# Kernel units that write one half of their products in reverse order, so that one VectorE copy collects a unit's results in place of two

## The chip, the cores and the metric

The kernel runs on one core of one Trainium2 chip. The metric is the device time of one execution in microseconds, taken as the median of the runs shown.

## What is computed

A tensor x of 2048 rows and 512 columns goes through two pairs of layers. Layer A is a two-dimensional Fourier filter, layer B a long convolution whose kernel K is built from complex exponentials. Cut to what matters:

```python
def _A_ref(x, w_r, w_i):
    X = rfft2(x) * (w_r + 1j * w_i)
    return irfft2(X, s=(S, D))

def _B_ref(u, A_re, A_im, B_re, B_im, C_re, C_im, log_dt, Dskip):
    dt = exp(log_dt)[:, None]
    logdA, dB, Cc = dt * (A_re + 1j * A_im), dt * (B_re + 1j * B_im), C_re + 1j * C_im
    P = exp(logdA[:, :, None] * arange(L)[None, None, :])
    K = einsum("dn,dnl,dn->dl", Cc, P, dB).real        # 512 channels, 128 states, 2048 taps
    y = irfft(rfft(pad(K)) * rfft(pad(u)))[:, :L]
    return y.T + u * Dskip

x = x + A(layernorm(x)); x = x + B(layernorm(x))
x = x + A(layernorm(x)); x = x + B(layernorm(x))
```

K does not depend on x, so it is built once and serves both B layers.

## The kernel before

The work is cut into small pieces, written as Python generators that yield the engine and the tile slots they want next. A planner, the class Clock, runs them on a model of the engines while the program is written: in each step it takes, among the pieces that could start within NEAR = 0.1 us of the earliest, the one with the lowest rank, lets it emit its next instructions, and charges them to the engine by the table COST (line 40). The order in which instructions stand in each engine's queue is what this planner chose. Two details of its model bear on the change: on GpSimd an element counts 2.12 ns, or 1.77 ns where no operand has more than one dimension longer than one (lines 365 to 367), and on VectorE 1.05 ns after a fixed 0.07 us. Where the model sees TensorE idle, the planner puts in filler matmuls (line 427) into a free PSUM bank.

There are two planner runs. The first (line 1379) interleaves the building of K with the first A layer; the second (line 1387) holds everything else.

K is built in 32 **kernel units** (unit_k, line 1237), each for 16 channels. Every time index is 64 times a coarse index plus or minus a fine one, so the exponentials are products of a first factor E1 (32 columns for each of 16 channels) and a second factor E2 with two halves h of 32 columns. In steps, with the lines:

1. TensorE forms phases in a two-bank PSUM tile p (lines 1244, 1245). ScalarE rounds them (1247), VectorE subtracts (1249) and takes the absolute value (1250), ScalarE takes two sines (1252, 1253): cosines into the SBUF tile c, sines back into p.
2. The magnitudes m come from exp_k (line 1233), 48 instructions on ScalarE.
3. The tile E holds real parts E[:, 0] and imaginary parts E[:, 1], each of 1536 columns: 512 for E1, 512 for half 0 and 512 for half 1 of E2. VectorE writes the imaginary parts (line 1260 for the first 1024 columns, line 1261 for half 1 with a minus sign), GpSimd the real parts (line 1264 for 1024 columns, line 1265 for half 1 with 512 columns).
4. TensorE multiplies E1 by E2 (line 1277: 32 products in the code, 64 in the trace) into a one-bank PSUM tile pk of kind "l". The kinds l, t, h and x share two such banks, so this tile competes with the folds and the inverse transforms of layer A for a place.
5. VectorE copies the 256 results of a partition from pk into KS, a buffer of 64 positions by 32 channels (lines 1284 to 1289). There are two copies of 128 columns, because half 0 belongs to the positions 32 to 63 in ascending order and half 1 to the positions 31 to 0 in descending order.
6. After eight units store_k (line 1291) writes KS to memory by four DMAs on SyncE's queue, and turn_k (line 1301) reads it back, transposes it and sends it on. There is one KS buffer; there are two E buffers.

The two lines that make the two copies:

```python
        for h, l in enumerate((slice(32, 64), slice(31, None, -1))):
            nc.vector.tensor_copy(KS[u // 8][:, l, o:o + 4].rearrange("p l e -> p e l"), k[:, :, h])
```

Beside the units, in the same planner run, layer A goes on: forward_a (line 581), first_a (line 710) with folds on TensorE (fold_d, line 636), products on VectorE (lines 744 to 746), one sum on GpSimd (line 750) and one on VectorE (line 752), and inv_a (line 776), whose sums stand on GpSimd (lines 803, 804) and whose results VectorE adds to x (lines 814, 816) before it takes their moments (540, 541). At the end norm_b (line 836) normalizes x for the first B layer (line 566). spectra_k (line 906) takes the spectrum of the finished part of K (lines 903, 925, 927).

Some pieces wait for the planner's own events: spread (line 544) for the moments of its rows, the copies that overwrite the folded buffer (lines 698, 772) for earlier folds. SBUF is cut by hand: one tensor wk of WORK columns holds rings of small buffers, of which RING1 serves the first planner run and RING2 the second.

Of the kernel before, what the change touches and what calls it, by code (L numbers as in the profile page):

```python
# [11 lines left out]
OP = mybir.AluOpType  # L12
# [1 line left out]
RING1 = {"co": (1024, 3), "si": (1024, 2), "oh": (1280, 1), "KS": (2048, 1), "KT": (512, 4), "yh": (512, 2), "gb": (256, 3), "st": (256, 2), "sk": (128, 1)}  # L14

RINGW = {"y": (516, 2), "d": (258, 3), "c": (256, 3), "a": (512, 2)}
RING2 = {"gi": (512, 8), "kh": (1024, 4), "yk": (1024, 2), "gk": (256, 2), "iy": (1024, 2)}

BANKS1, SAME1 = {'a': (0, 2, 4), 's': (6, 7)}, {'t': 's', 'h': 's', 'l': 's', 'x': 's', 'k': 'a'}
BANKS2 = {'x': (0, 1, 2, 3), 't': (4, 5), 'h': (6, 7), 'a': (0, 2, 4, 6), 'f': (0, 2)}  # L20
# [27 lines left out]
PACE = 0, 1  # L48
LATE = 1, 1
HOLD = 4  # L50
NEAR = 0.1
FILL = 1.5, 0.6, 0.22
LANES = 8

WORK = 16896


PSUM = bass.MemoryType.PSUM
# [135 lines left out]
class Clock:  # L194
# [4 lines left out]
    def __init__(self, net, last=None):  # L199
        self.net, self.n = net, len(net.nc.cur_bb.bb.instructions)  # L200
        self.free, self.seen, self.events, self.marks, self.drops = {}, {}, {}, [], []
        self.held, self.slots, self.land, self.piece, self.table, self.form = {}, {}, 0.0, None, "", None
        self.pools, self.lands, self.lanes = [], [], {}
        if last:
            self.lands = last.lands
            self.free, self.seen, self.events, self.land, self.table = last.free, last.seen, last.events, last.land, last.table

# [221 lines left out]

    def run(self, plan):  # L430

        pieces = [[rank, i, 0.0, (), piece] for i, (rank, piece) in enumerate(plan)]
        while pieces:
            ready = [(t, p) for p in pieces if (t := self.time(p[2], p[3])) is not None]
            assert ready, [p[4].__name__ for p in pieces]
            now = min(t for t, _ in ready) + NEAR
            t, p = min((e for e in ready if e[0] <= now), key=lambda e: e[1][:2])
            if any(isinstance(need, str) and "PE" in need.split() for need in p[3]):
                self.fill(t)
            self.piece = p[4]  # L440
            needs = next(p[4], self)
            end = self.note(t)
            if not (isinstance(needs, str) and needs[:1] == "+"):
                p[2] = end
            if needs is self:
                pieces.remove(p)
                self.drops += [k for k, h in self.held.items() if h[2] is p[4] and k not in self.drops]
            else:
                p[3] = needs if isinstance(needs, tuple) else () if needs is None else (needs,)
            self.release()  # L450


class Net:
# [81 lines left out]
    def moments(self, s2, st):  # L535

        nc = self.nc
        self.stat(st, s2 // 4)
        b = self.sm.tile([128, 6], F32, name="st")
        nc.vector.bn_stats(b, self.x[:, s2, :])  # L540
        nc.vector.bn_aggr(st[s2 // 4][0][:, s2 % 4, :], b)
        self.mark("moments", id(st), s2 // 4)

    def spread(self, i, st, act=False, half=None):

        yield "ACT", self.after(("moments", id(st), i), 4 if half is None else 2 * half + 2)
        mv, rs = (a if half is None else a[:, 2 * half:2 * half + 2] for a in st[i][:2])
        self.nc.scalar.activation(rs, mv[:, :, 1], AF.Sqrt, bias=1e-5)
        yield "DVE"
        self.nc.vector.reciprocal(rs, rs)  # L550
        if act:
            if len(st[i]) < 3:
                st[i] = *st[i], self.sm.tile([128, 4], F32, name="nb")
            b = st[i][2] if half is None else st[i][2][:, 2 * half:2 * half + 2]
            self.nc.vector.scalar_tensor_tensor(b, mv[:, :, 0], -1.0, rs, op0=OP.mult, op1=OP.mult)
        self.mark(*(k for k in (id(st), i, half) if k is not None))
# [74 lines left out]
    def fold_d(self, p, r, g):  # L631

        cs = p.rearrange("p (a b) -> p a b", a=2)
        for b, o in enumerate((cs[:, :, 0:64], cs[:, :, 64:128], p[:, 128:256], p[:, 384:512])):
            y = 2048 * b + 128 * g
            self.nc.tensor.matmul(o, self.Yf[r][:, y:y + 128], self.Da[:, b, :], start=True, stop=True)
        self.mark("fold", r)

    def group_a(self, g):

        nc = self.nc
# [8 lines left out]
        p = self.psum("t")  # L650
# [44 lines left out]
        for sg in range(2):  # L695
            nc.tensor.matmul(v[:, 2 + sg], Z[:, sg, 129:257], H[sg], start=True, stop=True)
        self.drop(Z, G)
        yield "ACT", self.emitted(("fold", 1), g // 4 * 4)
        nc.scalar.copy(Y1[:, 0:2], v[:, 0:2].rearrange("p b (s m) -> p b s m", s=16))
        P, M = (v[:, 2 + sg].rearrange("p (r s u) -> p r s u", r=2, s=16) for sg in range(2))  # L700
        yc, ys = Y1[:, 2:4, :, 0:4], Y1[:, 2:4, :, 4:8]
# [8 lines left out]
    def first_a(self, r, g):  # L710

        nc = self.nc
# [8 lines left out]
        p = self.psum("t")  # L721
# [36 lines left out]
        for b in range(2):  # L758
            o = v[:64, 128 * b:128 * b + 128]
# [3 lines left out]
            o = v[64:, 128 * b:128 * b + 128]  # L763
# [5 lines left out]
            nc.tensor.matmul(v[:, 256:512], Z[:, i, 129:257], ca[:, o:o + 2].rearrange("p a m -> p (a m)"),  # L769
                             start=i == 0, stop=i == 1)  # L770
        self.drop(Z, G)
        yield "ACT", self.emitted(("fold", r), g // 4 * 4)
        nc.scalar.copy(Y1, v.rearrange("p (b s m) -> p b s m", b=4, s=16))
        self.mark("group", r)

# [154 lines left out]
    def tables(self):  # L930

        for q in range(8):
            yield "+SP gi", self.emitted(("sent", 0), HOLD * (q > 1))
            self.gi[q] = self.w("gi", [128, 2, 8, 32])
# [131 lines left out]
    def moments_b(self, s2, e, st):  # L1066

        nc = self.nc
        yield "DVE", self.after(("summed", 0, e), self.returns(0, e)), self.emitted(("half", s2), e)
        if ("h", s2 // 4) not in st:  # L1070
            st["h", s2 // 4] = self.sm.tile([128, 4, 2, 6], F32, name="hm")
        m = st["h", s2 // 4][:, s2 % 4]
        nc.vector.bn_stats(m[:, e], self.x[:, s2, 256 * e:256 * e + 256])
        if e:
            nc.vector.bn_aggr(self.stat(st, s2 // 4)[:, s2 % 4, :], m.rearrange("p e m -> p (e m)"))
            self.mark("moments", id(st), s2 // 4)
        self.mark("half", s2)


# [157 lines left out]
    def unit_k(self, u, M, KS):  # L1237

        nc = self.nc
        b = u // 4  # L1240

        yield "PE p:a co si", self.emitted("exp", 6 * b + 6)
        p, c, s = self.psum("a"), self.w("co", [128, 1024]), self.w("si", [128, 1024])
        self.factors(p[:, :512], self.sq[b][:, 0], u, 0)
        self.factors(p[:, 512:], self.st[b], u, 2048)
        yield "ACT"
        nc.scalar.activation(c, p, AF.Identity, bias=MAGIC)  # L1247
        yield "DVE"
        nc.vector.scalar_tensor_tensor(s, c, MAGIC, p, op0=OP.subtract, op1=OP.subtract)  # L1249
        nc.vector.tensor_scalar(c.bitcast(U32), s.bitcast(U32), 0x7fffffff, None, op0=OP.bitwise_and)  # L1250
        yield "ACT"
        nc.scalar.activation(c, c, AF.Sin, scale=-TURN, bias=QUARTER)  # L1252
        nc.scalar.activation(p, s, AF.Sin, scale=-TURN)  # L1253
        self.drop(s)
        self.mark("front")
        yield "DVE E"

        m = M.pop(u)[:, u % 2]
        E = self.w("E", [128, 2, 1536])
        nc.vector.tensor_tensor(E[:, 1, :1024], p, m[:, :1024], op=OP.mult)  # L1260
        nc.vector.scalar_tensor_tensor(E[:, 1, 1024:], p[:, 512:], -1.0, m[:, 1024:], op0=OP.mult, op1=OP.mult)
        self.drop(p)
        yield "+ POOL"
        nc.gpsimd.tensor_tensor(E[:, 0, :1024], c, m[:, :1024], op=OP.mult)  # L1264
        nc.gpsimd.tensor_tensor(E[:, 0, 1024:], c[:, 512:], m[:, 1024:], op=OP.mult)
        self.drop(c)
        if u ^ 1 not in M:
            self.timer.drop_at(m, -1536 * (u % 2))
        yield "PE p:l" if u % 8 else "PE p:l KS", self.emitted("product", u)
        E1 = E[:, :, :512].rearrange("p r (i l) -> p r i l", i=16)  # L1270
        E2 = E[:, :, 512:].rearrange("p r (h i k) -> p r i h k", h=2, i=16)
        pk = self.psum("l")
        for e in range(4):
            for r in range(2):
                for j in range(4):
                    i = 8 * (e // 2) + 2 * j + e % 2
                    nc.tensor.matmul(pk[32 * j:32 * j + 32, 64 * e:64 * e + 64], E1[:, r, i, :], E2[:, r, i],  # L1277
                                     start=r == 0, stop=r == 1)
        if u % 8 == 0:
            KS[u // 8] = self.w("KS", [128, 64, 32])  # L1280
            self.timer.keep(KS[u // 8])
        self.drop(E)
        self.mark("product")
        yield "DVE", self.emitted("kernel", u)
        o = 4 * (u % 8)
        k = pk[:, :256].rearrange("p (e h k) -> p e h k", e=4, h=2)
        for h, l in enumerate((slice(32, 64), slice(31, None, -1))):
            nc.vector.tensor_copy(KS[u // 8][:, l, o:o + 4].rearrange("p l e -> p e l"), k[:, :, h])
        self.mark("kernel")

    def store_k(self, q, KS):
# [242 lines left out]
```

## Time and profile before

| | |
|---|---|
| median of 3 runs | 735.78 us (731.3 to 737.27) |
| the profiled execution's own time | 733.14 us |
| its span, first to last instruction | 731.4 us |
| its mean granted TensorE clock | 0.964 of full speed |
| first and last instruction of the kernel units' products on TensorE | 98.2 and 342.9 us from the start |

The time of an execution is the span and 1.74 us around it. In the trace the engines are PE (TensorE, with its weight loads apart as PEld), DVE (VectorE), ACT (ScalarE), POOL (GpSimd) and SP (SyncE, which issues DMAs); an engine's name with a q is its instruction queue. A row names a line of the kernel, the output and input buffers, and the shape. PE is busy for 84% of the span, DVE 75%, ACT 55%, POOL 45%; a busy PE also holds the fillers. Idle time of an engine is put down to the instruction that released it.

### The profile page before, as it was taken

How to read it: one execution, taken by the hardware profiler on the slowest of the kernel's cores; microseconds unless marked ns; L12 is line 12 of the kernel's file. 1: busy time of each engine (PE TensorE's matmuls, PEld its weight loads, DVE VectorE, ACT ScalarE, POOL GpSimd, SP SyncE). 2: the span in 40 equal slices, each digit the busy share in tenths (PEclk: the TensorE clock that was granted, in tenths of full speed). 3: DMA queues.
4: the chain of work that ended last, by engine and by line, in shares of the span. 5: the costliest groups of instructions: out<-in, count | busy, mean ns of one | idle time of the engine just before them, and what ended most of it. 6: DMA issues, size and time to landing. Idle time of an engine off the chain costs nothing. (4 is left out here: it accounts for less than half of the span.)

```text
span 731.4 us, 20387 instructions
## 1 busy us (share of the span) xinstructions
PE 611.0 (84%) x8490; PEld 408.8 (56%) x8490; DVE 546.7 (75%) x860; ACT 401.6 (55%) x660; POOL 332.7 (45%) x386
## 2 busy tenths in 40 slices
PE   4899799879987977878967889889998898688883
PEld 3888566645755554545623445578777675234341
DVE  5987396675966688979695799867666598697664
ACT  5677768858697858894403442057555265125320
POOL 4283073453544466546014645057656562066430
PEclk9899999989999999998999999989999999899997
DMA  9433421451324765434897444700378001488967
GB/s 326 139 110 114 130 88 59 114 153 52 103 75 126 228 204 156 146 125 150 267 339 238 151 147 136 287 1 1 123 264 286 2 18 72 145 241 278 364 170 218
DMA packets 96220, 116.06 MB, mean 159 GB/s; under 512 B 5660, under 2 KB 73248, under 8 KB 96000
## 3 DMA queue, kind: packets, MB, share of 16 engines
q1 hardware_dynamic: 75440, 100.08, 42.8%
q10 hardware_dynamic: 20688, 14.68, 6.4%
q8 instruction: 67, 1.10, 0.6%
q14 instruction: 25, 0.20, 0.1%
HBM read 79.22 MB, written 35.52 MB: 157 GB/s over the span
## 5 line engine op out<-in xcount | busy, mean ns | idle before, releaser
L981 POOL TENSOR_TENSOR apart<-wk 128x512 f32<-128x512 f32 x64 | 80.4, 1278 | 126.7 <-DVE wk L974 125.0
L974 DVE TENSOR_TENSOR wk<-ps,wk 128x1024 f32<-128x1024 f32 x64 | 74.8, 1212 | 19.7 <-PE ps L903 6.8
L1264 POOL TENSOR_TENSOR Y<-wk,Y 128x1024 f32<-128x1024 f32 x32 | 65.1, 2033 | 39.2 <-ACT wk L1252 23.2
L996 ACT COPY Y<-ps 128x512 f32<-128x512 f32 x64 | 34.6, 589 | 80.7 <-PE ps L991 60.0
L427 PE MATMUL ps<-cRa,cRb 128*128 128x128 f32 x582 | 75.4, 286 | 3.0 <-DMA cRb<-in_cRb_dram 3.0
L427 PEld LDWEIGHTS ps<-cRa,cRb 128*128 128x128 f32 x582 | 70.4, 199 | 12.5 <-issue 7.4
L1249 DVE SCALAR_TENSOR_TENSOR wk<-wk,ps 128x1024 f32<-128x1024 f32 x32 | 38.9, 1215 | 27.0 <-ACT wk L1247 26.7
L991 PE MATMUL ps<-apart,wk 32*64 32x256 f32 x1024 | 44.3, 396 | 10.6 <-POOL apart L981 5.7
L852 DVE STREAM_TRANSPOSE Y<-ps 128x1024 f32<-128x1024 f32 x24 | 44.1, 1917 | 10.6 <-PE ps L850 10.6
L1277 PE MATMUL ps<-Y 128*32 128x64 f32 x2048 | 39.3, 232 | 14.8 <-ACT wk L798 5.4
L591 POOL TENSOR_TENSOR wk<-wk 128x256 f32<-128x256 f32 x32 | 27.2, 848 | 52.2 <-ACT wk L564 26.1
L1277 PEld LDWEIGHTS ps<-Y 128*32 128x32 f32 x2048 | 33.3, 117 | 28.6 <-issue 7.6
L750 POOL TENSOR_TENSOR x<-x 128x257 f32<-128x257 f32 x16 | 10.2, 638 | 84.9 <-DVE x L745 84.9
L1233 ACT ACTIVATE Y<-ps 128x1024 f32<-128x1024 f32 x48 | 46.1, 1035 | 4.6 <-PE ps L1217 4.4
L609 PE MATMUL ps<-cRa,wk 128*128 128x256 f32 x128 | 37.1, 416 | 12.2 <-POOL wk L591 10.9
L1217 PE MATMUL ps<-wk,Y 96*128 96x512 bf16 x128 | 40.6, 398 | 6.9 <-DVE Y L1260 2.8
L903 PE MATMUL ps<-Y,wk 64*32 64x256 f32 x1024 | 35.8, 390 | 9.9 <-ACT Y L996 4.5
L1260 DVE TENSOR_TENSOR Y<-ps,Y 128x1024 f32<-128x1024 f32 x32 | 38.8, 1213 | 6.6 <-ACT ps L1253 6.5
L1252 ACT ACTIVATE wk<-wk 128x1024 f32<-128x1024 f32 x32 | 33.8, 1057 | 13.5 <-DVE wk L1250 13.4
L803 POOL TENSOR_TENSOR wk<-wk 128x256 f32<-128x256 f32 x32 | 22.7, 708 | 39.3 <-ACT wk L798 39.2
L991 PEld LDWEIGHTS ps<-apart,wk 32*64 32x64 f32 x1024 | 17.5, 130 | 38.5 <-POOL apart L981 25.4
L1247 ACT ACTIVATE wk<-ps 128x1024 f32<-128x1024 f32 x32 | 32.8, 1044 | 9.8 <-PE ps L1217 7.9
(207 smaller groups left out, 1615.1 us busy)
## 6 DMA issues: line engine op xcount, KB each, us to landing
wk<-khat SPq DMA_DIRECT2D x16, 512.0 KB, 8.0
wk<-yk SPq DMA_DIRECT2D x16, 512.0 KB, 6.3
Ya<-vd SPq DMA_DIRECT2D x16, 512.0 KB, 7.0
Y<-in_W_dram SPq DMA_DIRECT2D x12, 515.0 KB, 4.6
x<-in_cPa_dram SPq DMA_DIRECT2D x16, 384.0 KB, 3.1
yk<-wk SPq DMA_DIRECT2D x24, 256.0 KB, 2.3
Y<-in_cGa_dram SPq DMA_DIRECT2D x12, 384.0 KB
x<-in_W_dram SPq DMA_DIRECT2D x16, 258.0 KB, 3.3
```

The source lines that it names most:

```text
L427: self.net.nc.tensor.matmul(bank[:, :128], self.net.Rb, self.net.Ra[:, 1], start=True, stop=True)
L609: nc.tensor.matmul(p[:, 0:256], pq[:, 128 * i:128 * i + 128], R2[:, 128 * i:128 * i + 256], start=i == 0, stop=i == 1)
L852: self.nc.vector.transpose(self.place[e][:, :, 32 * i:32 * i + 32].rearrange("p k d -> p d k"), p.rearrange("p (w s d) -> p d s w", w=2, s ...
L974: nc.vector.tensor_tensor(t[c], x, kh[:, :, ::-1, :] if c else kh, op=OP.mult)
L981: nc.gpsimd.tensor_tensor(Z[:, :, c], t[0][:, :, c], t[1][:, :, c], op=op)
L991: nc.tensor.matmul(v[j][64 * a:64 * a + 64, h], gi[o:o + 32, j, 4 + 2 * c:6 + 2 * c, :].rearrange("p a m -> p (a m)"), Z[o:o + 32, j, c, : ...
L1217: self.nc.tensor.matmul(p, f[:, c:c + 128], self.oh[:k, o:o + 512], start=True, stop=True)
L1233: nc.scalar.activation(m[:, :, 1024:] if i == 2 else m[:, i, :1024], p.rearrange("p (i m) -> p i m", i=2) if i == 2 else p, AF.Exp)
L1249: nc.vector.scalar_tensor_tensor(s, c, MAGIC, p, op0=OP.subtract, op1=OP.subtract)
L1260: nc.vector.tensor_tensor(E[:, 1, :1024], p, m[:, :1024], op=OP.mult)
L1264: nc.gpsimd.tensor_tensor(E[:, 0, :1024], c, m[:, :1024], op=OP.mult)
L1277: nc.tensor.matmul(pk[32 * j:32 * j + 32, 64 * e:64 * e + 64], E1[:, r, i, :], E2[:, r, i], start=r == 0, stop=r == 1)
```

## The change

Line 1261 and line 1265, which write half 1 of E2, now write each row of 32 columns from its last column to its first. The products of half 1 then come out in the order of the positions 0 to 31, so both halves ascend, and one copy of 256 columns replaces the two of 128: its output steps backwards over the two halves, no longer over the columns. The instructions of the other lines of a unit are the same. Number of instructions per unit: one fewer on VectorE, the same on GpSimd.

Three changes beside it touch the planner or the layout. The events for moments and folds are counted by finer keys (by pairs of rows, and by groups of four folds). A table SHIFT can move a piece's rank; it is empty. The ring gk has buffers of 128 in place of 256 columns, which moves the ring iy 256 columns down, and WORK is 19072 in place of 16896 columns, so the tensors behind wk lie at other addresses.

```diff
-RING2 = {"gi": (512, 8), "kh": (1024, 4), "yk": (1024, 2), "gk": (256, 2), "iy": (1024, 2)}
+RING2 = {"gi": (512, 8), "kh": (1024, 4), "yk": (1024, 2), "gk": (128, 2), "iy": (1024, 2)}
+SHIFT = {}, {}
-WORK = 16896
+WORK = 19072
...
-        pieces = [[rank, i, 0.0, (), piece] for i, (rank, piece) in enumerate(plan)]
+        pieces = [[rank + SHIFT[self.part].get(i, 0), i, 0.0, (), piece] for i, (rank, piece) in enumerate(plan)]
...
-        self.mark("moments", id(st), s2 // 4)
+        self.mark("moments", id(st), s2 // 4, s2 % 4 // 2)
...
-        yield "ACT", self.after(("moments", id(st), i), 4 if half is None else 2 * half + 2)
+        yield "ACT", *(self.after(("moments", id(st), i, h), 2) for h in ((0, 1) if half is None else (half,)))
...
         self.mark("fold", r)
+        self.mark("fold", r, g // 4)
...
-        yield "ACT", self.emitted(("fold", 1), g // 4 * 4)
+        yield "ACT", self.emitted(("fold", 1, g // 4 - 1), 4 * (g > 3))
...
-        yield "ACT", self.emitted(("fold", r), g // 4 * 4)
+        yield "ACT", self.emitted(("fold", r, g // 4 - 1), 4 * (g > 3))
...
         nc.vector.tensor_tensor(E[:, 1, :1024], p, m[:, :1024], op=OP.mult)
-        nc.vector.scalar_tensor_tensor(E[:, 1, 1024:], p[:, 512:], -1.0, m[:, 1024:], op0=OP.mult, op1=OP.mult)
+        back = E[:, :, 1024:].rearrange("p r (i k) -> p r i k", i=16)[:, :, :, ::-1]
+        pairs = [t.rearrange("p (i k) -> p i k", i=16) for t in (p[:, 512:], c[:, 512:], m[:, 1024:])]
+        nc.vector.scalar_tensor_tensor(back[:, 1], pairs[0], -1.0, pairs[2], op0=OP.mult, op1=OP.mult)
...
         nc.gpsimd.tensor_tensor(E[:, 0, :1024], c, m[:, :1024], op=OP.mult)
-        nc.gpsimd.tensor_tensor(E[:, 0, 1024:], c[:, 512:], m[:, 1024:], op=OP.mult)
+        nc.gpsimd.tensor_tensor(back[:, 0], pairs[1], pairs[2], op=OP.mult)
...
         k = pk[:, :256].rearrange("p (e h k) -> p e h k", e=4, h=2)
-        for h, l in enumerate((slice(32, 64), slice(31, None, -1))):
-            nc.vector.tensor_copy(KS[u // 8][:, l, o:o + 4].rearrange("p l e -> p e l"), k[:, :, h])
+        nc.vector.tensor_copy(KS[u // 8][:, :, o:o + 4].rearrange("p (h k) e -> p e h k", h=2)[:, :, ::-1], k)
```

## The prediction on record

> **What bounds the kernel now.** I began with the busy time of each engine in the stretch that holds all kernel units, 85 to 345 us, to see whether one engine sets its length.
>
> ```profile
> core 0: us, PE busy (x) PEld busy (x) DVE busy (x) ACT busy (x) POOL busy (x), PEclk, DMA share, GB/s
> 85.00:345.00 260.00, 219.76 (x3599) 146.26 (x3599) 200.00 (x327) 199.09 (x250) 132.47 (x124) 0.95 0.41 125
> 345.00:731.40 386.40, 323.73 (x4459) 202.97 (x4457) 289.73 (x436) 145.91 (x326) 164.91 (x208) 0.97 0.55 179
> ```
>
> None does. VectorE and ScalarE work 200 and 199 of the 260 us (77%), GpSimd 132 (51%), TensorE 220 (85%). Of the 220 a part is filler, by the same view for line 427 alone (the first pair of numbers is PE, the second PEld):
>
> ```profile
> 85.00:345.00 260.00, 18.33 (x144) 16.93 (x145) 0.95 0.41 125
> ```
>
> Without the 18.33 us of filler TensorE has 201 us (77%). Three engines with a quarter of their time free: the stage is set by hand-overs between them, in an order that the planner fixed. The other 386 us contain no line that the change's arithmetic touches. So I read the waits of the stage next (us in total, times, longest).
>
> ```profile
> POOL x L750 <- DVE x L745: 70.6, 8, 15.4
> DVE wk L1249 <- ACT wk L1247: 26.7, 7, 10.3
> POOL Y L1264 <- ACT wk L1252: 23.2, 6, 6.7
> ACT wk L1252 <- DVE wk L1250: 13.4, 11, 2.9
> DVE wk L1288 <- PE ps L1277: 10.0, 9, 2.8
> PEld ps L1277 <- POOL Y L1265: 7.6, 9, 1.9
> PE ps L1277 <- POOL Y L1265: 3.1, 4, 1.7
> ```
>
> The reader is to see three things. A unit's products on TensorE (L1277) wait for GpSimd's second product (L1265) in 9 of 32 units by the weight loads. The copies (L1288) wait for TensorE in 9 units, and in the others stand behind VectorE's own work. And in 11 units ScalarE waits for a late VectorE (L1252 for L1250).
>
> **The copies on VectorE.** First the line of the copies by itself, then two neighbours of it and two lines that give a slope.
>
> ```profile
> L1288 DVE COPY wk<-ps x64: 358/380/419, 100.2 to 343.4; 128x128 f32<-128x128 f32 x64
> ...
> 210.18 0.60 DVE L1288 COPY wk<-ps 128x128 f32<-128x128 f32 x2
> 210.62 0.41 DVE L752 TENSOR_TENSOR x<-x 128x257 f32<-128x257 f32 x1
> ...
> L1260 DVE TENSOR_TENSOR Y<-ps,Y 128x1024 f32<-128x1024 f32 x32 | 38.8, 1213 | 6.6 <-ACT ps L1253 6.5
> ...
> L1261 DVE SCALAR_TENSOR_TENSOR Y<-ps,Y 128x512 f32<-128x512 f32 x32 | 21.7, 678 | 0.0
> ```
>
> One copy lasts 380 ns, but a pair only 0.60 us, not 0.76: the second starts before the first has ended. The instruction behind the pair starts 0.44 us after it began, so a pair occupies VectorE for 0.44 us and one copy for 0.22. An element costs (1213 - 678) / 512 = 1.045 ns, so 128 more in one copy cost 0.134 us. One copy of 256 then lasts 0.38 + 0.134 = 0.514 us and occupies 0.22 + 0.134 = 0.354. Per unit VectorE gains 0.44 - 0.354 = 0.086 us and the result is there 0.60 - 0.514 = 0.086 us earlier; over 32 units **2.8 us of VectorE time**. The busy-time sum of the page will fall by more, since it counts the overlap twice: 64 x 0.381 = 24.4 us of durations become 32 x 0.514 = 16.4.
>
> Bounds: the most that can go is the whole second copy, 0.22 x 32 = 7.0 us. On the other side, if the scattered elements of these copies cost (380 - 143) / 128 = 1.85 ns (143 ns is what line 1261 has left at 1.045 an element), the new copy lasts 0.617 us, 0.017 later than the pair: 0.5 us lost over 32 units. I take 2.8, since the pair's own start distance of 0.22 us leaves little room for 1.85 ns an element.
>
> **VectorE's reversed write (L1261).** No row shows VectorE writing with a step of -1. The nearest are the two copies of line 1288, of which one writes ascending and the other descending: all 64 lie between 358 and 419 ns, so a direction costs or saves at most 0.06 us, 2 us over 32 units either way. I take 0: the input of the instruction is unchanged, and line 1260's count per element holds.
>
> **GpSimd's reversed write (L1265).** This is the price that matters, and no row has it. The rows of GpSimd, min/median/max in ns:
>
> ```profile
> L1265 POOL TENSOR_TENSOR Y<-wk,Y x32: 1082/1092/1616, 94.0 to 338.5; 128x512 f32<-128x512 f32 x32
> ...
> L1264 POOL TENSOR_TENSOR Y<-wk,Y x32: 1992/1998/2242, 91.9 to 336.6; 128x1024 f32<-128x1024 f32 x32
> ...
> L684 POOL TENSOR_TENSOR Ya<-Ya x15: 1271/1278/1292, 519.4 to 572.3; 128x514 f32<-128x514 f32 x15
> ...
> L595 POOL TENSOR_TENSOR wk<-wk x16: 457/465/1440, 10.6 to 58.0; 128x129 f32<-128x129 f32 x16
> ...
> L596 POOL TENSOR_TENSOR wk<-wk x16: 450/460/913, 11.0 to 58.8; 128x128 f32<-128x128 f32 x16
> ```
>
> Line 596 reads both inputs backwards and line 595 forwards: 460 and 465 ns for 128 and 129 elements, so direction is free on the reading side, and I take it as free on the writing side. But the new operands are 16 rows of 32, where line 1265 so far ran over one flat row. Line 684 works on two rows of 257 and takes 1278 ns for 514 elements, the flat line 1265 takes 1092 for 512: rows cost 0.186 us. I take **0.186 us a unit, 6.0 us of GpSimd time** over 32, by the thought that the extra belongs to the elements. Bounds: nothing below (0 us), and above, if it belongs to each row start, 0.186 / 2 = 0.093 a row, 1.49 us for 16 rows, 47.6 us over 32 units.
>
> The Trainium skill speaks to this: its GPSIMD Engine Reference, section Elementwise — side-by-side cycle accounting, has the address pattern done in hardware at no cycles per element, and the two inputs' shared read port as what limits a sum of two tensors. By it the second product would stay at 1092 ns and this term would be 0. The rows of lines 684 and 1265 differ by 0.186 us at the same size, so the trace does not bear it out for patterns with two rows, and I keep the row's price.
>
> **The shared wait of VectorE and GpSimd.** A longer GpSimd instruction also lasts into more of line 1250, which reads and writes SBUF on VectorE:
>
> ```profile
> L1250 DVE TENSOR_SCALAR wk<-wk x32: 694/696/2534, 87.7 to 333.7; 128x1024 uint32<-128x1024 uint32 x32
> ...
> 333.72 1.63 DVE L1250 TENSOR_SCALAR wk<-wk 128x1024 uint32<-128x1024 uint32 x1
> ...
> 332.80 2.00 POOL L1264 TENSOR_TENSOR Y<-wk,Y 128x1024 f32<-128x1024 f32 x1 [0.63 <-ACT wk L1252]
> 334.76 1.54 POOL L1265 TENSOR_TENSOR Y<-wk,Y 128x512 f32<-128x512 f32 x1
> ...
> L1250 DVE TENSOR_SCALAR wk<-wk 128x1024 uint32<-128x1024 uint32 x32 | 30.0, 938 | 2.6
> ```
>
> The instance at 333.72 us lasts until 335.35, about 0.55 us past the end of line 1264 at 334.80, and line 1265 behind it takes 1.54 in place of 1.09. Over 32 units line 1250 loses (938 - 696) x 32 = 7.7 us. GpSimd's two products grow from 1998 + 1092 to 3276 ns, by 6%, so I add 0.06 x 7.7 = **0.5 us of VectorE time**. The Trainium skill's SBUF — State Buffer, section Who interferes with whom, calls the port pair of VectorE and GpSimd an exclusive lock whose loser waits for the whole instruction; the rows at 333.72 and 334.76 us agree, and the new copy, which reads PSUM as the old ones did, stays as free of it as they are (419 ns at most).
>
> **What of it reaches the end.** VectorE's gain counts where another engine waits for VectorE: ScalarE in 11 units, 11 x 0.086 = 0.95 us earlier. GpSimd's loss counts where TensorE waits for line 1265, 9 units, and the copies wait for TensorE in as many: 9 x 0.186 = 1.67 us later. In the other 23 units the product's place in TensorE's queue, or VectorE's line 1261, covers it; without that cover it would be the whole 6.0. Of the lock 11/32 x 0.5 = 0.17 counts. Behind the last unit both vanish:
>
> ```profile
> 343.14 0.60 DVE L1288 COPY wk<-ps 128x128 f32<-128x128 f32 x2 [0.35 <-PE ps L1277]
> ...
> 343.77 4.20 SPq L1297 DMA_DIRECT2D kd<-wk  x4
> 348.07 8.26 SPq L927 DMA_DIRECT2D khat<-wk  x5
> ...
> 357.41 0.57 SPq L1308 DMA_DIRECT2D wk<-kd  x1
> ```
>
> The store of the last KS is released by the last copy, but its reader on the same queue stands behind five other transfers until 357.41. No wait and no DMA is added.
>
> Sum: -0.95 + 1.67 + 0.17 = **+0.9 us**. The profiled execution's 733.14 becomes 734.0; it lies 2.6 us below the median of the runs, 735.78, and I carry the 0.9 over to that: **736.7 us**, no change.
>
> **The rest of the diff.** SHIFT is empty: 0. The finer keys ask for the same folds and moments as long as folds and rows come in order, which their rising ranks make so: 0. The ring iy moves by 256 columns onto buffers whose last use, the transfers of line 927 until 356.3, is past when turn_k's last reads begin at 357.41, ahead of the writes to iy: 0, and a wait of one transfer, 8.26 / 5 = 1.7 us, if that cover were gone. WORK moves tensors to other addresses; no row prices an address, so 0.
>
> **What I can't sum: the order.** The planner counts line 1265 with 1.23 us in place of 1.05 (2.12 for 1.77 ns an element, as the pattern has two long dimensions) and the copies with 0.34 in place of 0.41. Both shifts are about the size of its window of 0.1 us, 32 times over, so pieces will change places, in the second run too. What one exchange is worth I bound by the longest waits of the stage that lie on a unit's path: 10.3 us (line 1249 for 1247), either way.
>
> **The rivals.** (1) *Faster*: the order falls so that one such wait closes, and VectorE's gain is at its bound, 11 x 0.22 = 2.4 us in place of 0.95: 736.7 - 10.3 - 1.5 = 724.9 us. For it: 77% busy engines leave room, and 11 late line-1250 instructions are hurt by VectorE alone. Against: TensorE's waits name GpSimd oftener than VectorE. (2) *Slower by the order*: one more wait of 10.3 us, 736.7 + 10.3 = 747.0 us. For it: a later line 1265 keeps E, of which there are two, longer. Against: GpSimd is only 51% busy. (3) *Slower by the rows*: GpSimd pays 0.093 us for each of 16 row starts, at line 1265. Then it takes 2.58 us; the nine waiting units lose 9 x 1.49 = 13.4 us in place of 1.67, which gives 748.4 us, and if the other 23 pass on half of their 34.3 us, 765.6 us. It decides from an extra of about 0.8 us a unit on, where 9 x 0.8 = 7.2 us is the 1%. For it: no row has 16 short rows. Against: two rows cost only 0.186 in all. (4) *The change doesn't save what it says*: the copy of 256 costs as long as the pair, since pairs overlap already; the time is then 736.7 + 0.95 = 737.6, within the forecast.
>
> **How the numbers follow.** No change, with (4) in it: 0.54, from 729 to 743. Rival (1): 0.23. Rival (2): 0.18. Rival (3): 0.05. A measurement of this kernel can tell about 1% from no change; the three runs spread by 6 us. So faster by over 1% 0.23, within 1% 0.54, slower by over 1% 0.23. The range takes in (1) and (2) to just beyond their middle and the lower case of (3), which leaves about 2 in 10 out: 724 to 749.
>
> **What would show it.** In the new profile: line 1288 once a unit with about 510 ns (350 or 620 would refute the slope); line 1265's successor at about 1280 ns (1090 would say that patterns are free, over 1900 that rows are dear); line 1261's at 678. The waits of TensorE for GpSimd's second product should grow by under 2 us in all. If the time moves by more than 7 us while these durations come out as said, the order did it, and the waits for line 1247 and line 1252 should have changed. The forecast is wrong if GpSimd comes to be the most frequent releaser of TensorE in the stage, or if the second half of the kernel changes length.

## The result and the profile after

| | before | after |
|---|---|---|
| median of the runs measured side by side (20 each) | 737.05 us | 731.21 us |
| ratio, 95% interval | | 0.9935, 0.9914 to 0.9956 |
| profiled execution: time, span, granted clock | 733.14, 731.4, 0.964 | 729.39, 727.3, 0.960 |

The changed kernel is faster by 0.65%, about 4.8 us. The ratio is taken over the fast runs alone (one of before's took 1925.75 us), so it is not the quotient of the two medians. The forecast was 736.7 us, 0.9 us longer than before and called no change; a kernel faster by its order stood only in rival (1), at 724.9 us. So the direction is wrong, though the time lies in the range and within the 1% called "no change".

The unit's lines moved by some places: L1282 is now the products on TensorE, L1292 the one copy, L1266 the reversed product on VectorE, L1269 and L1270 GpSimd's two products, L1253 the absolute value, L429 the fillers. First the lines of the changed instructions in the profile of after (min/median/max in ns), then the copy with the instruction behind it (start, length in us), then the grouped rows of the stage from 85 to 345 us (busy us, mean ns, idle time ahead).

```profile
L1292 DVE COPY wk<-ps x32: 580/607/637, 100.7 to 341.4; 128x256 f32<-128x256 f32 x32
...
L1270 POOL TENSOR_TENSOR Y<-wk,Y x32: 1083/1093/1627, 93.2 to 337.5; 128x512 f32<-128x512 f32 x32
...
L1266 DVE SCALAR_TENSOR_TENSOR Y<-ps,Y x32: 669/676/682, 92.5 to 337.9; 128x512 f32<-128x512 f32 x32
```
```profile
100.66 0.62 DVE L1292 COPY wk<-ps 128x256 f32<-128x256 f32 x1
101.10 0.43 DVE L755 TENSOR_TENSOR x<-x 128x257 f32<-128x257 f32 x1
```
```profile
L1253 DVE TENSOR_SCALAR wk<-wk 128x1024 uint32<-128x1024 uint32 x32 | 29.9, 935 | 2.6
L1292 DVE COPY wk<-ps 128x256 f32<-128x256 f32 x32 | 19.3, 604 | 13.8 <-PE ps L1282 5.2 <-ACT Y L1236 3.3 <-ACT wk L1250 2.7
```

Three things are to be seen. The one copy lasts 0.62 us and the next instruction starts 0.44 us behind its start: the pair had 0.60 and the same 0.44, so VectorE won no time. GpSimd's product, whose output is now 16 rows of 32 written backwards, has 1093 ns where the flat one had 1092. The absolute value, L1253, which the prediction expected to wait longer for GpSimd, has a mean of 935 ns (938). None of the changed instructions became cheaper or dearer. Now the stage, first in busy time (PE, PEld, DVE, ACT, POOL, clock, DMA share), then the waits.

```profile
85.00:345.00 260.00, 217.59 (x3605) 145.71 (x3606) 200.67 (x296) 201.81 (x253) 133.55 (x125) 0.95 0.43 127
345.00:727.30 382.30, 320.42 (x4393) 199.68 (x4391) 288.42 (x436) 145.27 (x324) 163.53 (x206) 0.96 0.55 179
```
```profile
POOL x L753 <- DVE x L748: 43.1, 4, 14.5
DVE wk L1252 <- ACT wk L1250: 39.3, 10, 9.3
...
POOL Y L1269 <- ACT wk L1255: 11.0, 6, 5.4
...
DVE wk L1292 <- PE ps L1282: 5.2, 7, 1.7
...
PEld ps L1282 <- POOL Y L1270: 3.5, 3, 1.4
```

VectorE's busy time in the stage is the same (200.67 after 200.00), but the waits were dealt anew: GpSimd for VectorE 43.1 us where it was 70.6, VectorE for ScalarE's rounding 39.3 (26.7), GpSimd for the sine 11.0 (23.2), the copies for TensorE 5.2 (10.0). Instructions of the same durations wait in other places, which is what another order looks like. The queues of the two traces do differ. In the first planner run TensorE's and ScalarE's part by single exchanges from about the fourth unit on (109 and 115 us), VectorE's and GpSimd's from behind the 13th (about 195 us); the sums of layer A on VectorE, the line that was 814, begin at 243.7 in place of 255.6 us. The second run differs by some exchanges. The order also changes what comes with it: ScalarE has 21 table loads (ACT_TABLE_LOAD, 1283 ns each) in the stage where it had 19, about the 2.7 us that its busy time grew, and TensorE has 526 filler instructions in the whole trace where it had 582.

### The profile page after: what moved, and what is told of

The parts are those of the page before. It is cut to its first block, busy times and chain, and to the rows that moved or that the text cites. A ratio compares the mean times of both kernels' runs of the same rounds, so it can differ in the third digit from the quotient of the medians.

```text
span 727.3 us, 20233 instructions
## 1 busy us (share of the span) xinstructions
PE 605.8 (83%) x8434; PEld 403.4 (55%) x8434; DVE 545.9 (75%) x828; ACT 404.8 (56%) x662; POOL 333.1 (46%) x386
## 3 DMA queue, kind: packets, MB, share of 16 engines
q1 hardware_dynamic: 75440, 100.08, 43.1%
## 5 line engine op out<-in xcount | busy, mean ns | idle before, releaser
L984 POOL TENSOR_TENSOR apart<-wk 128x512 f32<-128x512 f32 x64 | 80.2, 1278 | 126.9 <-DVE wk L977 109.4
L1269 POOL TENSOR_TENSOR Y<-wk,Y 128x1024 f32<-128x1024 f32 x32 | 65.0, 2032 | 36.4 <-ACT wk L1255 11.0
L429 PE MATMUL ps<-cRa,cRb 128*128 128x128 f32 x526 | 67.8, 286 | 2.8 <-DMA cRb<-in_cRb_dram 2.8
L429 PEld LDWEIGHTS ps<-cRa,cRb 128*128 128x128 f32 x526 | 63.8, 199 | 11.2 <-issue 6.3
L1252 DVE SCALAR_TENSOR_TENSOR wk<-wk,ps 128x1024 f32<-128x1024 f32 x32 | 38.9, 1214 | 39.4 <-ACT wk L1250 39.3
L1282 PE MATMUL ps<-Y 128*32 128x64 f32 x2048 | 37.1, 227 | 11.2 <-DVE x L819 4.1
L1282 PEld LDWEIGHTS ps<-Y 128*32 128x32 f32 x2048 | 31.9, 114 | 25.6 <-issue 17.7
L906 PE MATMUL ps<-Y,wk 64*32 64x256 f32 x1024 | 35.8, 390 | 9.2 <-DVE Y L855 3.9
L811 PE MATMUL ps<-wk,cRaT 128*128 128x384 f32 x64 | 29.8, 548 | 11.7 <-POOL wk L807 5.6
```

Of the source, the lines that this page charges most:

```text
L429: self.net.nc.tensor.matmul(bank[:, :128], self.net.Rb, self.net.Ra[:, 1], start=True, stop=True)
L984: nc.gpsimd.tensor_tensor(Z[:, :, c], t[0][:, :, c], t[1][:, :, c], op=op)
```

## The experiments

Theories. **Order**: the planner's two changed charges (1.23 for 1.05 us on GpSimd, 0.34 for 0.41 on VectorE) made it write another order, and that order is faster. **Instructions**: the one copy or the earlier result saves time by itself. **Layout**: the finer keys, the ring and the addresses do it. All ratios below are to the kernel before, run beside it on the same chip. "Order" means all that the planner decides: the sequence in each queue, the places of tiles, and the fillers.

### Instructions against order

`new_old_plan` has after's code, but the planner charges the new instructions as the old ones, so that the queues come out as before's. `old_new_plan` has before's instructions and charges them as the new ones: after's queues.

```diff
 new_old_plan
-if all(sum(b > 1 for _, b in a.ap[1:]) < 2 for a, _ in aps):
+if all(sum(b > 1 for _, b in a.ap[1:]) < 2 for a, _ in aps) or [b for _, b in out.ap[1:]] == [16, 32]:
...
+if [b for _, b in out.ap[1:]] == [4, 2, 32] and ins.opcode != "StreamTranspose": fixed += 0.07
 old_new_plan
+if all(sum(b > 1 for _, b in a.ap[1:]) < 2 for a, _ in aps) and n != 512:
...
+if [b for _, b in out.ap] == [128, 4, 32]: fixed -= 0.035
```

> The changed kernel with all its instructions, but the planner is told to charge the new copy and GpSimd's second product what it charged the old ones, so every queue has the order of before. Order theory (the gain comes from the planner's new order, the instructions themselves save nothing): within 0.2% of before, about 737 us, with the new copy at about 604 ns as in the changed kernel. Direct theory (one copy in place of two saves VectorE time that the stage passes on): 0.993 of before, about 732 us. Layout theory (other addresses and rings): 0.993 too, and then the kernel with the layout alone shows it.

> The instructions of before (two copies, forward writes), in the order of the changed kernel: the planner charges line 1265 at 2.12 ns an element and each of the two copies half of what it charges the one. Order theory: 0.9935 of before, about 732 us, like the changed kernel. Direct theory: 737 us, within 0.2% of before. Layout theory: 737 us.

`rest_only` is after without the edit of the unit (old products, two copies); `unit_only` is before with that edit alone.

> Everything of the change but the unit's edit: finer keys, ring gk of 128, WORK of 19072; the queues keep the order of before. Order theory and direct theory: within 0.2% of before, about 737 us. Layout theory: 0.993 of before, about 732 us.

> The unit's edit alone on the kernel before (keys, gk and WORK as before); its queues have the order of the changed kernel. Order theory and direct theory: 0.9935 of before, about 732 us. Layout theory: 737 us, no gain.

| | instructions | order of | ratio | 95% interval |
|---|---|---|---|---|
| new_old_plan | new | before | 1.0045 | 1.0018 to 1.0073 |
| old_new_plan | old | after | 0.9920 | 0.9892 to 0.9948 |
| rest_only | old, with the rest of the diff | before | 0.9998 | 0.9975 to 1.0021 |
| unit_only | new, without the rest | after | 0.9930 | 0.9905 to 0.9954 |

The old instructions in the new order have the whole gain; the new ones in the old order are slower, if anything; the rest of the diff does nothing. The order theory holds, the other two fall. The granted clock does not make the gain: it was 0.959 in the mean of old_new_plan's runs and 0.961 in before's beside them. The grouped row of the copy in new_old_plan shows the same 0.60 us, so the copy's price doesn't depend on the order:

```profile
L1294 DVE COPY wk<-ps 128x256 f32<-128x256 f32 x32 | 19.2, 601 | 14.8 <-PE ps L1284 10.7 <-ACT wk L1252 3.2 <-ACT Y L1238 0.9
```

### Which planner run

Here the planner's decisions were written down and played back with before's instructions: the first run in after's order and the second in before's, and the reverse.

```diff
+ORDER = "<first run's decisions>", "<second run's decisions>"
...
+if self.script:
+    i = int(self.script.pop(0)[1:])
+    t, p = next(e for e in ready if e[1][1] == i)
```

> The instructions of before; the planner's first run (kernel units and first A layer) is replayed in the order of the changed kernel, its second run in the order of before. If the gain is made in the stage that holds the kernel units: 0.993, about 732 us. If it is made in the second run, as the single profiles suggest (the changed kernel is 0.8 us ahead at the start of the first B layer, of 4.1 at the end): 0.999, about 736 us.

> The instructions of before; first planner run in the order of before, second run in the order of the changed kernel. If the gain is made in the second run: 0.994 to 0.996, about 733 us. If in the stage of the kernel units: 1.000, 737 us.

first_new: 0.9936 (0.9904 to 0.9968). second_new: 1.0009 (0.9982 to 1.0036). The gain is in the order of the first run, which holds the units and ends at about 355 us; the second's exchanges are worth nothing that can be measured.

### Why the one copy is as long as two

The copy writes KS with the position innermost: each element lands 32 channels, 128 bytes, from the one ahead of it. This kernel has after's instructions in before's order and walks the four adjacent channels innermost, so that four elements in a row fill 16 adjacent bytes.

```diff
-nc.vector.tensor_copy(KS[u // 8][:, :, o:o + 4].rearrange("p (h k) e -> p e h k", h=2)[:, :, ::-1], k)
+nc.vector.tensor_copy(KS[u // 8][:, :, o:o + 4].rearrange("p (h k) e -> p h k e", h=2)[:, ::-1], k.rearrange("p e h k -> p h k e"))
```

> The changed kernel's instructions in the order of before, but the copy walks its 256 elements with the four adjacent channels innermost, so it writes runs of 16 bytes in place of single elements 128 bytes apart, and reads PSUM in steps. If the scattered writes make the copy slow (1.75 ns an element): the copy falls from 604 to about 510 ns and the next instruction starts about 0.35 us after it in place of 0.44; time 0.998 to 1.002 of the kernel before. If reading in steps costs as much or the writes are not the cause: 600 ns or more, time about 1.004 as with the other walk.

The grouped row and the first copy's place in the timeline:

```profile
L1294 DVE COPY wk<-ps 128x256 f32<-128x256 f32 x32 | 13.5, 420 | 17.1 <-PE ps L1284 11.0 <-ACT wk L1252 4.0 <-ACT Y L1238 1.0
```
```profile
99.79 0.42 DVE L1294 COPY wk<-ps 128x256 f32<-128x256 f32 x1
100.12 0.42 DVE L757 TENSOR_TENSOR x<-x 128x257 f32<-128x257 f32 x1
```

420 ns in place of 601, and VectorE is occupied for 0.33 us in place of 0.44, with the same 256 elements from the same bank. The scattered write was the price; the reads now step 256 bytes from element to element, and the copy is shorter all the same. By the Trainium skill's SBUF — State Buffer, section Specifications (TRN2), a line of SBUF has 16 bytes and a walk needs two hits or more on a line for full bandwidth; 601 against 420 ns agree with it. This copy saves what the change was written to save, 0.11 us a unit or 3.5 us of VectorE's time, and more than the 2.8 forecast; the kernel's ratio is 0.9994 (0.9961 to 1.0027). In this order VectorE's time in the units buys nothing that can be measured.

### Other orders

If an order that nobody aimed at gains 0.65%, others should move the time as well. charge_pool is before with one number in the planner: GpSimd's second product is charged at 2.12 ns an element. charge_2_3 charges 2.30. e_inner_pool_plan has after's code, the fast copy, and charge_pool's order. e_inner_true_plan has the same code and charges what was measured: 1.77 ns on GpSimd, and one copy, without the 0.07 us that the other two kernels with the fast copy add so as to keep a given order.

```diff
 charge_pool
+if all(sum(b > 1 for _, b in a.ap[1:]) < 2 for a, _ in aps) and n != 512:
 charge_2_3
-        each = 1.77
+        each = 2.30 if n == 512 else 1.77
```

> The instructions of before, all three of them; only the planner's charge for GpSimd's second product is raised from 1.77 to 2.12 ns an element, which gives a third order. If the gain comes from what this charge says of the chip (the planner leaves GpSimd more time): about 0.993, 732 us. If the gain is the luck of one order among many: anything from 0.99 to 1.01, no reason for 0.993.

> The instructions of before, all of them; only the planner's charge for GpSimd's second product is raised further, from 1.77 to 2.30 ns an element, a fifth order. If the gain comes from giving GpSimd more time in the plan, more is as good or better: 0.988 or less. If orders are luck: anything from 0.988 to 1.005.

> The changed kernel's instructions with the faster walk of the copy (420 ns), in the order that the raised charge for GpSimd alone gave (0.988 of before with the old instructions). If the 0.11 us that this copy saves on VectorE in each unit reaches the end: 0.984, about 725 us. If order is all: 0.988, 728 us.

> The changed kernel's instructions with the faster walk of the copy, and the planner charges what the traces show: 1.77 ns an element for GpSimd's second product, 0.34 us for the copy. If a truer charge makes the better order: 0.988 or less, 728 us or less. If orders are luck: anything from 0.988 to 1.005.

| | instructions | ratio | 95% interval |
|---|---|---|---|
| charge_pool | old | 0.9881 | 0.9839 to 0.9924 |
| charge_2_3 | old | 0.9969 | 0.9938 to 1.0000 |
| e_inner_pool_plan | new, fast copy | 0.9879 | 0.9830 to 0.9928 |
| e_inner_true_plan | new, fast copy | 0.9903 | 0.9865 to 0.9941 |

The four other orders that the planner wrote (after's among them, and the last one with the new instructions) are all at or below before's in time; before's is the slowest of the five. One number in a table, with no instruction of the layers changed, gains 1.2% (727.27 us), twice what the change gains. The truest charges give 0.9903, no better than a wrong one, so the accuracy of the charges is not what sets these orders apart. The fast copy adds nothing to charge_pool's order that can be measured (0.9879 beside 0.9881, with intervals of half a percent, as large as the 3.5 us in question): e_inner_pool_plan, at 725.88 us, is the fastest kernel of this study by median, and as far as can be measured the order alone accounts for that.

A rival is the number of fillers, since before's order has the most: 582 filler instructions in the trace, against 526 in after, 542 in charge_pool and 516 in charge_2_3. The kernel no_late_fills of the next section has before's order with 528, and before's time (1.0008), so the number by itself is not the cause.

### Where in the first run's order

A suspicion came from the hand-over to the next stage. First ScalarE and TensorE in before (start, length, what ended the wait), then in after.

```profile
354.47 1.27 ACT L925 COPY wk<-ps 128x512 f32<-128x512 f32 x2 [1.43 <-PE ps L903]
356.32 1.21 ACT L866 COPY wk<-ps 128x512 f32<-128x512 f32 x2 [0.58 <-PE ps L834]
```
```profile
349.97 3.39 PE L427 MATMUL ps<-cRa,cRb 128*128 128x128 f32 x28
353.29 1.09 PE L903 MATMUL ps<-wk 64*32 64x256 f32 x32
355.11 3.95 PE L834 MATMUL ps<-Ya,cRb 64*128 64x512 f32 x15 [0.72 <-ACT wk L925]
```
```profile
347.51 1.09 PE L906 MATMUL ps<-wk 64*32 64x256 f32 x32
348.54 1.13 PE L837 MATMUL ps<-Ya,cRb 64*128 64x512 f32 x4
```
```profile
352.66 1.08 ACT L869 COPY wk<-ps 128x512 f32<-128x512 f32 x2
```

In before TensorE spends 3.39 us in fillers and takes the last spectrum (L903) at 353.29, and the next stage's first products (L834) wait for that spectrum's copy. In after the last spectrum (L906) is done at 348.6, ahead of the last four normalizations in the order, and the next stage starts at 348.54; its first copies on ScalarE come 3.7 us earlier. The first guess was the fillers: no_late_fills is before's order without the first run's last three filler blocks (27 matmuls in the code).

> The instructions and orders of before, replayed, but without the last three blocks of filler matmuls of the first planner run (27 in the code), which stand ahead of the last two spectra of K on TensorE's queue. Hand-over theory (in the order of before the last spectra end after the last normalization and hold ScalarE and a PSUM bank that the first B layer wants): the distance from the last normalization to the first transpose of the B layer falls from 5.9 us to 4.5 or less, time 0.997 to 0.999. Otherwise: 5.9 us as before and 1.000.

1.0008 (0.9976 to 1.0040), and the distance that was to fall to 4.5 us is 8.8 us in its profile. The theory of the fillers falls. Then the order itself was cut: before's order up to a step, and from there what is left in after's order (tail), or the reverse (head). Step 688 is about 186 us, 900 about 267, 1100 about 330.

```diff
-ORDER = "<before's first run>", "<before's second run>"
+ORDER = "<first n decisions of one order, then the remaining ones in the other's sequence>", "<before's second run>"
```

> The instructions of before throughout; the second planner run in before's order; in the first planner run the order of before for its first 688 planner steps (up to the copies of the 13th kernel unit, about 186 us in the trace of before) and from there the order of after. The whole first run in the order of after gave 0.9936. If the gain arises anywhere behind 186 us: 0.990 to 0.997. If it arises in the exchanges of the 13 units before that: 1.000 +- 0.003.

> The opposite: the order of after for the first 688 steps, before's from there, second run as in before. If the gain arises behind 186 us: 1.000 +- 0.003; if ahead of it: 0.990 to 0.997.

> As the first of these kernels, with the change of order only from step 900 on (the copies of the 23rd unit, about 267 us). If the gain arises in the last units and in the hand-over to the next stage (345 to 360 us): 0.990 to 0.997. If it is gathered between 186 and 267 us, where inv_a starts 12 us earlier in after: 1.000 +- 0.003.

> As above, from step 1100 on only (the copies of the 29th unit, about 330 us): what changes place is the end of layer A and the last spectra, which stand ahead of the last four norm_b in place of behind them. If the place of the last spectra at the hand-over is the cause: 0.990 to 0.997, and the distance from the last norm_b to the first transpose of x falls from 5.9 us to below 5. If it is not: 1.000 +- 0.003.

tail_687 1.0091 (1.0059 to 1.0122), head_687 1.0099 (1.0068 to 1.0130), tail_900 1.0168 (1.0132 to 1.0203), tail_1100 1.0079 (1.0049 to 1.0108): all slower, which no theory had. The waits for the fillers (L450 there) say why; the row is that of tail_1100 between 320 and 375 us (us in total, times, longest).

```profile
PE ps L450 <- ACT ps L1269: 6.4, 1, 6.4
```

A filler that is played back writes the PSUM bank that was recorded for it. Behind the seam that bank was not free any more: ScalarE's second sine (L1269) still had its tile there, and TensorE's whole queue stood behind a filler that computes nothing: 6.4 us in tail_1100, tail_900 and tail_687, 4.4 in head_687. The four runs therefore measure the seam and not only the order. The wait alone doesn't cover the 12 us of tail_900; its runs also had a clock of 0.950 where before's had 0.961. The last two runs leave the first run's fillers behind the seam out, for tail_687 and tail_1100. (The texts on record for them say 13.3 and 13.1 us; those sums held the wait of the weight load, 7.0 and 6.6 us, and that of the matmul, 6.4 in both, which are one and the same time, so 7.0 and 6.6 at most are meant.)

> As the kernel that follows the order of after from step 688 on (1.0091), but without the filler matmuls of the first planner run behind the seam. In that kernel TensorE stood 13.3 us in two filler blocks that waited for a PSUM bank which ScalarE's second sine still held, and the last unit's copies came 8 us late. If the order behind 186 us carries the gain and those fillers hid it: 0.990 to 0.997. If a spliced order is slower by itself: above 1.003.

> The same for the seam at step 1100 (about 330 us; with fillers 1.0079, 13.1 us of TensorE's time in such waits). If the hand-over at 345 to 360 us carries the gain: 0.990 to 0.997; if it is gathered between 186 and 330 us: 1.000 +- 0.003; if a spliced order is slower by itself: above 1.003.

tail_687_nf: 0.9961 (0.9928 to 0.9995). tail_1100_nf: 0.9952 (0.9916 to 0.9987). Both are faster than before, and the intervals hold the 0.9936 of the whole first run. So the part from 330 us on, the end of layer A with the hand-over, carries 0.48 of the 0.64% by the middle values. That the missing fillers do it is unlikely for tail_1100_nf, since no_late_fills leaves out 27 of the 32 that before has behind that step and gains nothing; for tail_687_nf, which lacks more of them, there is no such control. What this leaves open: the intervals are as wide as the difference between "most" and "all", and no single exchange of the hand-over was tried by itself.

The traces' own distance from the start of the last normalization to the start of the first transposition of the next stage is 5.9 us in before and 5.0 in after. The other profiles bear out that it goes with the order: 5.3 to 9.9 us in the seven kernels with before's order at the end of the first run, 2.8 to 5.1 in the nine with after's, 2.7 to 3.4 in the four with the other planner orders. In before and after it is 0.9 us of the 4.8; the rest can't be placed from single profiles, since two with the same queues (before and rest_only) differ by 7 us in span (731.4 and 738.4).

## Why the prediction was wrong

**The step that failed is "What I can't sum: the order".** It saw that the planner charges two instructions otherwise, named the consequence (pieces change places, in both runs) and the bound (10.3 us either way), and then left it out of the sum as if its mean were zero, without a reason. It was the only term that counted: 0.9920 with the old instructions in the new order. The gain was made in the first planner run (0.9936 by itself); the second run's exchanges, which the prediction also named, gave 1.0009. Its sign stood in no row of before's profile: which order is faster was seen only by running it. But before's order is one among many, and the five that the planner wrote here differ by 1.2% (0.988 to 1.000), so "within 1%" was less likely than the chance it was given. Which exchange makes this order faster stays open.

**The rival.** Rival (1), faster by the order, had the mechanism, at 724.9 us. Its own picture, one wait of 10.3 us that closes, was not what happened: the longest wait of VectorE for the rounding is still 9.3 us, and that wait grew in sum (39.3 after 26.7). About 4.8 us came in place of 11.8 (736.7 - 724.9).

**VectorE's copies: -2.8 us of VectorE, -0.95 of the time.** Mis-sized. The slope of 1.045 ns an element came from instructions that write adjacent elements. The copy of 128 with a scattered write has 381 ns and that of 256 has 604: (604 - 381) / 128 = 1.74 ns an element, near the text's other bound of 1.85. Rival (4), the copy costs as long as the pair, was true, and its 0.54 shared with the forecast hid that: it changes the term to 0. The argument against the bound, that the pair's start distance leaves little room, compared a distance with a duration: the copy of 256 also overlaps its successor by 0.18 us. The page's busy time doesn't count such an overlap twice, as the prediction had it: it shows 19.4 us for the 64 old copies, not 24.4, and 19.3 for the 32 new ones.

**VectorE's reversed write: 0.** Right: 676 ns where 678 stood.

**GpSimd's reversed write: +0.186 us a unit, +1.67 of the time.** Mis-sized: +0.001 us. The prediction says that the new operands are 16 rows of 32; only the output is. The two inputs, `c[:, 512:]` and `m[:, 1024:]`, are 512 adjacent columns however they are written, and the trace's record of L1270 has them as one run of 512. Line 684, two rows of 257 in all three operands, was therefore no neighbour. Nor do rows explain its price; the rows of before, min/median/max in ns:

```profile
L981 POOL TENSOR_TENSOR apart<-wk x64: 1262/1278/1297, 380.3 to 704.5; 128x512 f32<-128x512 f32 x64
...
L591 POOL TENSOR_TENSOR wk<-wk x32: 718/750/1708, 9.9 to 505.3; 128x256 f32<-128x256 f32 x32
...
L750 POOL TENSOR_TENSOR x<-x x16: 631/638/644, 67.4 to 241.3; 128x257 f32<-128x257 f32 x16
```

Line 981 also has two rows, of 256, and also takes 1278 ns; but line 591, one flat run of 256, takes 750 ns where line 750, one flat run of 257, takes 638. What the slower ones pay for was not tried. The Trainium skill's GPSIMD Engine Reference, section Elementwise — side-by-side cycle accounting, gives address generation no cycles per element; for the pattern of the output 1093 beside 1092 ns agree with it, and the pattern of the inputs did not change here. Rival (3) falls with the term.

**The lock: +0.17.** The mean of the absolute value is 935 ns after 938: 0, as GpSimd's product did not grow.

**The rest of the diff: 0.** Right: 0.9998 for rest_only.

**The sum.** With the three terms at their measured sizes it is 0 in place of +0.9; that two wrong prices nearly cancelled, and so left "no change" for the instructions, was luck. The instructions alone measured 1.0045, slower by 0.18 to 0.73%, which no term explains. The record points to the clock: new_old_plan's runs had a mean granted clock of 0.956, the 35 runs of before beside them 0.961, and a line fitted through those 35 has a time longer by 3.9 us for a clock lower by 0.01. That makes about 2 of the 2.6 us between the two means (739.8 and 737.2 us). With the faster copy in the same order the ratio is 0.9994, at a clock of 0.960 in both. By the same relation the gain of the two kernels without fillers (0.955 and 0.956 beside 0.961) would grow by some 2 us, to the size of the whole first run's, and part of why charge_2_3 gains less (0.954 beside 0.960) may be the clock. Why the clock was lower in these runs, by chance or by the kernel, isn't shown.

**What would show it.** The copy at 607 ns stands by the 620 that the text gave as refuting the slope, the GpSimd line at 1093 said that patterns are free (1090). The order was to be the cause if the time moved by more than 7 us, and the waits for lines 1247 and 1252 were then to change: the time moved by less, and these waits changed all the same, 26.7 to 39.3 and 23.2 to 11.0. The threshold was too high for a cause that was there. TensorE's waits for GpSimd's second product, which were to grow, fell (the weight loads' from 7.6 to 3.5 us). A second half of another length was to be a sign of being wrong: it went from 386.40 to 382.30 us in the profiles, and the two profiles of one order, before and rest_only, differ by more, so that sign can't be read from one profile.

## What to carry to other kernels

Where a planner or a scheduler places instructions by a cost table, every edit is two edits: the instruction, and the order that its charge brings about. Take them apart before you credit the instruction, by running the new instructions with the old charges and the old ones with the new charges; and ask first what a few arbitrary orders of the unchanged kernel cost, for a gain within that spread says nothing of the edit. Price an instruction from a row with the same walk of each operand, not only the same engine and count. Before a difference of half a percent is explained, set the runs' granted clocks beside their times.

## What the runs showed of the hardware

- A VectorE copy of 256 f32 of a partition from PSUM takes 604 ns when each element lands 128 bytes from the last, and 420 ns when four in a row fill 16 bytes. Two copies of 128 with the scattered walk take 0.60 us as a pair, since the second starts 0.22 us behind the first.
- GpSimd's product of two flat f32 runs of 512, written as 16 rows of 32 backwards, takes 1093 ns, as one written flat (1092). A sum or difference over two rows of 256 takes 1278 ns.
- By a line through 35 runs of the kernel before on one chip, a granted TensorE clock lower by 0.01 goes with a time longer by 3.9 us (0.5%).
- A filler matmul isn't free where its PSUM bank is held: in the four spliced orders TensorE stood for 4.4 to 6.4 us in front of one, and they ran 0.8 to 1.7% longer than before; without fillers behind the seam two of them ran 0.4 and 0.5% shorter than before.
